# Expert tiles from an earlier point on, summary copies ahead of loads, and one exponential over two PSUM banks in a fused attention and mixture-of-experts kernel

## The chip, the cores and the metric

The kernel runs on one core of a Trainium2 chip. The metric is the device time of one execution in microseconds (us), lower is better. With one core there are no two dies to compare, so "slow" here only marks a run that is over 1.5% above the fastest run of the same kernel in its set of runs; all others are "fast". Executions of one kernel scatter by up to 4% within a set, and chips differ, so kernels are compared through ratios to the kernel before in the same set of runs. A ratio is the mean time of one kernel's fast runs over the mean of the other's fast runs of the same rounds, so it is not quite the ratio of the medians that stand beside it.

## The reference, cut to what matters

```python
# attention: q, k, v are (4, 8, 768, 64)
k_sum = k.reshape(B, H, 24, 32, D).max(axis=3)      # a summary of each block of 32 keys
v_sum = v.reshape(B, H, 24, 32, D).mean(axis=3)
# scores to the keys nearer than 16, and to the 24 summaries (+ log 32); one softmax over both
...
# mixture of experts on the 3072 tokens, width 512, 8 experts, hidden width 1024
logits = x @ w_gate + modality_bias[modality_id]
e_idx = np.argmax(logits, axis=1)
...
for e in range(E):
    h = np.maximum(x[mask] @ w1[e], 0.0)
    out[mask] = gate_w[mask, None] * (h @ w2[e])
```

## The kernel before

The program walks over 16 pairs of heads, four to a batch. After the last pair of a batch the batch is routed: each token gets its expert and a row in a DRAM buffer `xs` sorted by expert, and six indirect DMAs (scatters) write the tokens there. A "list" then names tiles of 256 rows with one expert. A tile is a generator; one step of it is a "unit", and `UNITS` says at which of six places of a pair one unit is run between attention work. What no unit took is run after the last pair (the tail).

```python
def scores(n, half):
    ...
    pss = [bank([128, 6, 64], FP32, f"pss{h}") for h in range(2)]   # one of 8 shared banks each
    ...
    for h in range(2):
        nc.scalar.activation(pT[:, h], pss[h], AF.Exp, scale=SCALE)

def tick(m=1):                       # one of 8 places in a pair
    ticks[0] += 1
    if ticks[0] % 2 == 0:
        scatter()                    # one scatter at every second tick
    for _ in range(m):               # m steps of the route
        while side and next(side[0], side) is side:
            side.popleft()

def rows(lst, j, i):                 # rows of tile i, issued by SP
    ...
    nc.sync.dma_start(xr.bitcast(I32), xs[ds(row, 256)].rearrange(...))

def weights(lst, j, i):              # the tile's expert, if another one than is there
    ...
    load_weights(i % NWB, e, cond=go > 0)        # both matrices, issued by GpSimd

def weights_ahead(n):                # guessed experts of tiles 0 and 1, by halves p0 to p7
    for p in {n + 2: (n,) for n in range(8)}.get(n, ()):
        ...
        if p == 3:
            guessed[0] = 1
        if p == 7:
            guessed[0] = NTILE + NWB
            ahead()                              # calls weights() of tile 1

for n in range(np_):
    scores(n, 1)
    tick(2 if n >= 8 else 1)
    pump(u[0])                                   # a unit of a tile, or none
    keys(n + 2)                                  # its halo copies on GpSimd
    ...                                          # at the first pair of a batch: start its route
    load(n + 4)                                  # three DMA issues on GpSimd
    weights_ahead(n)
    ...
    values(n, 0)
    ...
    summaries(n + 2)                             # two DVE reductions, one copy on GpSimd
    ...
    queries(n + 2); blocks(n + 1); scores(n + 1, 0); features(n - 1); values(n, 1)
    if n in ENLIST:                              # (7, 10, 14)
        scatter(NC)
        enlist(lists[b - 1])                     # row loads, weights
```

The softmax here doesn't subtract the row's maximum and nothing guards it: scores larger than these inputs give would overflow.

Of the kernel before, what the change touches and what calls it, by code (L numbers as in the profile page):

```python
# [10 lines left out]
FP32 = mybir.dt.float32  # L11
I32 = mybir.dt.int32
U32 = mybir.dt.uint32
AF = mybir.ActivationFunctionType
# [8 lines left out]
def kernel(  # L23
# [12 lines left out]
    nc = tc.nc  # L36
# [27 lines left out]
    ctx.enter_context(tc.manual_schedule())  # L64

    def bank(shape, dt, name):
        return ps.tile(shape, dt, tag="b", bufs=8, name=name)


    NMASK = 9  # L70
    NV, NK = 6, 3
    kvs = [const.tile([128, 2, NT, 128], FP16, name=f"kv{i}") for i in range(NK)]
    vbs = [const.tile([128, NT, 2, D + 1], FP16, name=f"vb{i}") for i in range(NK)]
# [26 lines left out]

    def borders(i):
        kv, vb = kvs[i], vbs[i]
        nc.vector.memset(kv[:, :, 0, 64:80], 0.0)
        nc.vector.memset(kv[:, :, NT - 1, 80:96], 0.0)
        nc.vector.memset(kv[:, :, :, KR:128], 0.0)
        nc.vector.memset(vb[0:WK, :, :, D:D + 1], 1.0)
        nc.vector.memset(vb[WK:KR, :, :, D:D + 1], 32.0)

    borders(0)
    tok = const.tile([128, NJ], I32, name="tok")  # L110
    nc.gpsimd.iota(tok, pattern=[[128, NJ]], base=0, channel_multiplier=1)
    midc = const.tile([NJ, 128], mybir.dt.int64, name="midc")
    mb0 = const.tile([128, 2, E], FP32, name="mb0")
    nc.sync.dma_start(mb0, moe_modality_bias.unsqueeze(0).to_broadcast([128, 2, E]))
# [44 lines left out]
    w1b = [wpool.tile([128, NCD, F], FP16, name=f"w1b{i}") for i in range(NWB)]  # L159
    w2b = [wpool.tile([128, NF, DM], FP16, name=f"w2b{i}") for i in range(NWB)]  # L160
    guess = const.tile([128, NWB], I32, name="guess")

    def early_constants():
        nc.vector.tensor_scalar(erev, cidx[:, 0:E], -1.0, float(E), op0=ALU.mult, op1=ALU.add)
        g1 = work.tile([128, 2], FP32, tag="g1", bufs=1, name="g1")
        nc.vector.reduce_max(g1, mb0, axis=AX.X)
        nc.vector.memset(exl, -1.0)
        yield

        g2 = work.tile([128, 2, E], FP32, tag="g2", bufs=1, name="g2")  # L170
        nc.vector.tensor_tensor(g2, mb0, g1.unsqueeze(2).to_broadcast([128, 2, E]), op=ALU.is_ge)
        nc.vector.memset(done, 0.0)
        nc.vector.tensor_tensor(g2, g2, erev[:, None, :].to_broadcast([128, 2, E]), op=ALU.mult)
        yield
        nc.vector.reduce_max(g1, g2, axis=AX.X)
        nc.vector.memset(ones, 1.0)
        nc.vector.tensor_tensor(exl[:, 0:1], g1[:, 0:1], g1[:, 1:2], op=ALU.max)
        nc.vector.tensor_tensor(exl[:, 1:2], g1[:, 0:1], g1[:, 1:2], op=ALU.min)
        yield
        nc.vector.tensor_scalar(exl[:, 0:2], exl[:, 0:2], -1.0, float(E), op0=ALU.mult, op1=ALU.add)  # L180
        nc.vector.tensor_copy(guess, exl[:, 0:2])
        yield

    def later_constants():
        nc.vector.tensor_scalar(erow, cidx[:, 0:E], float(RP), 256.0, op0=ALU.mult, op1=ALU.add)
        nc.vector.memset(xrs[-1], 0.0)
        nc.sync.dma_start(xs[0:256].rearrange("(a p) d -> p a d", p=128), xrs[-1].bitcast(I32))
        yield
        nc.gpsimd.dma_start(wg, moe_w_gate.rearrange("(c p) e -> p c e", p=128))
        yield  # L190
        nc.vector.tensor_scalar(upper, cidx, pidx, None, op0=ALU.is_gt)
        nc.vector.tensor_copy(prow[:, 0:1], pidx)
        nc.vector.tensor_scalar_add(prow[:, 1:2], pidx, 128.0)
        yield
        nc.vector.tensor_scalar_mul(k256, cidx[:, 0:KM].unsqueeze(2).to_broadcast([128, KM, E]), 256.0)
        nc.vector.tensor_tensor(rowc, k256, erow[:, None, :].to_broadcast([128, KM, E]), op=ALU.add)
        yield
        nc.vector.tensor_copy(tab[:, 2], cidx[:, None, 0:E].to_broadcast([128, KM, E]))
        mdiff = work.tile([128, E], FP32, tag="mdiff", bufs=1, name="mdiff")
        nc.vector.tensor_tensor(mdiff, mb0[:, 1, :], mb0[:, 0, :], op=ALU.subtract)  # L200
        yield
        mh = work.tile([NJ, 128], FP16, tag="mh", bufs=1, name="mh")
        nc.vector.tensor_copy(mh, midc.bitcast(I32)[:, 0::2])
        for _ in range(4):
            yield
        pm = bank([128, NJ], FP16, "pm")
        nc.tensor.transpose(pm, mh, ident[0:NJ, 0:NJ])
        yield
        midf = work.tile([128, NJ], FP32, tag="midf", bufs=1, name="midf")
        nc.vector.tensor_copy(midf, pm)  # L210
        yield
        nc.vector.tensor_tensor(base, midf.unsqueeze(2).to_broadcast([128, NJ, E]),
                                mdiff[:, None, :].to_broadcast([128, NJ, E]), op=ALU.mult)
        yield
        nc.vector.tensor_tensor(base, base, mb0[:, 0:1, :].to_broadcast([128, NJ, E]), op=ALU.add)
# [48 lines left out]
    def blocks(n):  # L264

        kv, vb = st[n]["kv"], st[n]["vb"]
        for half in range(2):
            pv = bank([128, 6, 128], FP16, "pv")
            for tl in range(6):
                nc.tensor.transpose(pv[:, tl, :], kv[:, 1, 6 * half + tl, :], ident)  # L270
            (nc.vector.tensor_copy if half or n < NMASK and n % 2 else nc.scalar.copy)(  # L271
                vb[0:KR, 6 * half:6 * half + 6, :, 0:D],
                pv[0:KR].rearrange("p t (h d) -> p t h d", h=2))

    def scores(n, half):
        s = st[n]
        qT, kv = s["qT"], s["kv"]
        pss = [bank([128, 6, 64], FP32, f"pss{h}") for h in range(2)]
        if n < NMASK:
            for h in range(2):  # L280
                nc.tensor.matmul(pss[h], ident, bterm[:, 6 * half:6 * half + 6, :],
                                 start=True, stop=False, skip_group_check=True)
        for tl in range(6):
            t = 6 * half + tl
            for h in range(2):
                rr = slice(64 * h, 64 * h + 64)
                nc.tensor.matmul(pss[h][:, tl, :], kv[rr, 0, t, :],  # L287
                                 qT[rr, ts(t, 8), :].rearrange("p s c -> p (s c)"),
                                 start=n >= NMASK, stop=True, skip_group_check=True)
        pT = work.tile([128, 2, 6, 64], FP16, tag="pT", bufs=3, name="pT")  # L290
        for h in range(2):
            nc.scalar.activation(pT[:, h], pss[h], AF.Exp, scale=SCALE)  # L292
        if n >= NMASK:
            nc.vector.tensor_tensor(  # L294
                pT[0:WK], pT[0:WK],
                bmask[0:WK, None, 6 * half:6 * half + 6, :].to_broadcast([WK, 2, 6, 64]), op=ALU.mult)
        s["pT", half] = pT
# [254 lines left out]



    UNITS = {9: "000111", 10: "101111", 11: "111111", 12: "101111", 13: "111111", 14: "111111", 15: "101111"}
    ENLIST = (7, 10, 14)
    todo, pending, heads = deque(), deque(), set()
    ended, guessed = [0], [0]

# [50 lines left out]

    def weights_ahead(n):

        for p in {n + 2: (n,) for n in range(8)}.get(n, ()):
            if p % 4 == 0:
                gv[p // 4] = nc.gpsimd.value_load(guess[0:1, p // 4:p // 4 + 1], min_val=0, max_val=E - 1)
            load_weights(p // 4, gv[p // 4], which=(p // 2 % 2,), part=p % 2)
# [4 lines that stand above are left out]
                ahead()  # L621
# [1 line left out]
    keys(0)  # L623
    summaries(0)
    load(2)
    borders(1)
    queries(0)
    scores(0, 0)
    blocks(0)
    keys(1)  # L630
    summaries(1)
    load(3)
    borders(2)
    queries(1)
    side.append(early_constants())
    side.append(later_constants())
    for n in range(np_):
        b, cc = pairs[n]
        u = [int(c) for c in UNITS.get(n, "000000")]
        scores(n, 1)  # L640
        tick(2 if n >= 8 else 1)
        pump(u[0])
        if n + 2 < np_:
            keys(n + 2)
        if n and cc == 0:
            features(n - 1)
            assert not side
            side.append(route(b - 1))
        if n + 4 < np_:
            load(n + 4)  # L650
        weights_ahead(n)
        tick(2 if n >= 8 else 1)
        pump(u[1])
        values(n, 0)
        tick(2 if n >= 8 else 1)
        if n + 2 < np_:
            summaries(n + 2)
        tick(2 if n >= 8 else 1)
        pump(u[2])
        if n + 2 < np_:  # L660
            queries(n + 2)
        tick(2 if n >= 8 else 1)
        pump(u[3])
        if n + 1 < np_:
            blocks(n + 1)
            tick(2 if n >= 8 else 1)
            scores(n + 1, 0)
        tick(2 if n >= 8 else 1)
        pump(u[4])
        if cc:  # L670
            features(n - 1)
        tick(2 if n >= 8 else 1)
        values(n, 1)
        tick(2 if n >= 8 else 1)
        if n in ENLIST:
            assert not side
            scatter(NC)
# [55 lines left out]
```

## Time and profile before

| | before |
|---|---|
| time, median of the first set of runs | 233.67 us (233.24 to 236.83, 4 runs) |
| span of the profiled run | 228.3 us |
| busy: PE, DVE, ACT, POOL | 184.0, 122.8, 119.4, 124.9 us |
| PE busy share | 81% |
| first expert matmul | 86.12 us |
| last features of attention | 155.15 us |

A pair is read from its second score matmuls to those of the next pair. Pair 7 starts at 58.69 us, and 79.8 us remain from the start of pair 15 to the end. The lengths of the pairs and the views are in the prediction below. No engine but TensorE is busy for more than 55% of the span; that is an average, and before 91 us single stretches are fuller (VectorE 8.99 of 9.30 us from 44.8 us on, DMA engines at a share of about 1).

### The profile page before, as it was taken

The page shows a single profiled execution, that of the slowest core. Times are in us where ns is not written, and L with a number is a line of the kernel's source. Part 1 is how long each engine was busy: PE and PEld are TensorE (multiplying, and loading weights), DVE is VectorE, ACT ScalarE, POOL GpSimd, SP SyncE. Part 2 cuts the span into 40 slices and gives each one's busy share as a digit, 9 for nine tenths or more (in the row PEclk, how much of TensorE's full clock was granted, in tenths as well). Part 3 has the DMA queues.
Part 4 walks back from the last instruction along what each step waited for, and adds up shares of the span by engine and source line. Part 5 has one row for each costly group of instructions (what it writes and reads, how often), then busy time and mean ns, then how long its engine had stood idle before and what let it go on. Part 6 is the DMA issues. An engine that isn't in the chain of part 4 may idle for free. (4 is left out here: it accounts for less than half of the span.)

```text
span 228.3 us, 6765 instructions
## 1 busy us (share of the span) xinstructions
PE 184.0 (81%) x2720; PEld 131.5 (58%) x2720; DVE 122.8 (54%) x352; ACT 119.4 (52%) x207; POOL 124.9 (55%) x198
## 2 busy tenths in 40 slices
PE   0676797869696549999789999999959899999900
PEld 0464575667465536766577667576626667766500
DVE  6369979699958994655449763534870111101000
ACT  2586568576854441867457675462424255554410
POOL 8459529738889180498531575311574757372220
PEclk9999589967977575999999999999997999999985
DMA  5979929999999999139950123241121434312100
GB/s 76 136 106 139 188 44 143 187 205 172 203 221 153 227 172 160 37 88 207 200 198 3 70 100 136 81 143 47 69 103 56 157 118 141 112 51 83 52 19 0
DMA packets 20090, 27.44 MB, mean 120 GB/s; under 512 B 2876, under 2 KB 16468, under 8 KB 20052
## 3 DMA queue, kind: packets, MB, share of 16 engines
q0 software_dynamic: 17424, 24.40, 52.8%
q1 hardware_dynamic: 2628, 2.54, 4.0%
q8 instruction: 23, 0.38, 0.7%
q14 instruction: 15, 0.12, 0.2%
HBM read 85.46 MB, written 10.44 MB: 420 GB/s over the span
## 5 line engine op out<-in xcount | busy, mean ns | idle before, releaser
L530 PE MATMUL ph<-xg,w1b 128*128 128x256 f16 x416 | 53.8, 285 | 6.6 <-DVE at L516 3.8
L530 PEld LDWEIGHTS <-w1b 128*128 128x128 f16 x416 | 40.4, 101 | 14.9 <-issue 7.0
L542 PE MATMUL pmo<-w2b,hT 128*128 128x512 f16 x208 | 48.5, 379 | 0.0
L548 POOL DMA_INDIRECT out_dram<-ot,at x26 | 25.9, 997 | 32.8 <-ACT ot L547 22.3
L292 ACT ACTIVATE pT<-pss 128x384 f16<-128x384 f32 x64 | 28.0, 495 | 23.5 <-PE pss L287 23.4
L533 ACT ACTIVATE hT<-ph 128x512 f16<-128x512 f32 x52 | 30.6, 602 | 17.2 <-PE ph L530 16.7
L547 ACT ACTIVATE ot<-pmo,xr 128x512 f32<-128x512 f32 x26 | 17.9, 688 | 27.7 <-PE pmo L542 18.0
L351 POOL DMA_INDIRECT xs<-xb,posi x24 | 24.9, 1040 | 13.1 <-issue 5.3
L542 PEld LDWEIGHTS <-hT 128*128 128x128 f16 x208 | 19.2, 98 | 20.6 <-ACT hT L533 1.4
L238 ACT COPY kv<-pk 128x768 f16<-128x768 f16 x32 | 24.3, 810 | 8.1 <-PE pk L237 7.8
L513 DVE COPY xg<-px 128x1024 f16<-128x1024 f16 x13 | 8.9, 686 | 34.0 <-PE px L511 34.0
L270 PE MATMUL pv<-ident,kv 128*128 128x128 f16 x192 | 16.0, 244 | 4.0 <-POOL kv L251 4.0
L318 DVE TENSOR_TENSOR xb<-po,rec 128x384 f16<-128x384 f32 x32 | 17.8, 557 | 1.0
L241 POOL COPY kv<-kv 128x352 f16<-128x352 f16 x16 | 7.9, 493 | 18.7 <-ACT kv L238 18.5
L270 PEld LDWEIGHTS <-kv 128*128 128x128 f16 x192 | 13.5, 110 | 5.7 <-POOL kv L251 4.4
L248 DVE TENSOR_REDUCE ks<-kv 128x24 f16<-128x768 f16 x16 | 15.1, 944 | 2.2 <-ACT kv L238 2.2
L250 DVE TENSOR_REDUCE ks<-kv 128x24 f16<-128x768 f16 x16 | 15.1, 943 | 0.8 <-ACT kv L238 0.8
L294 DVE TENSOR_TENSOR pT<-pT,bmask 96x768 f16<-96x768 f16 x14 | 8.5, 604 | 13.2 <-ACT pT L292 13.2
L330 DVE COPY xT<-pt 128x768 f16<-128x768 f16 x16 | 8.9, 555 | 12.0 <-PE pt L327 11.8
L271 DVE COPY vb<-pv 120x768 f16<-120x768 f16 x20 | 10.7, 551 | 7.4 <-PE pv L270 7.4
L261 ACT COPY qT<-pq 128x768 f16<-128x768 f16 x16 | 12.9, 809 | 3.0 <-PE pq L259 2.9
L287 PEld LDWEIGHTS <-kv 64*128 64x128 f16 x384 | 8.4, 101 | 10.4 <-issue 8.9
(127 smaller groups left out, 280.7 us busy)
## 6 DMA issues: line engine op xcount, KB each, us to landing
w1b<-in_moe_w_dram POOLq DMA_DIRECT2D x13, 1024.0 KB
w2b<-in_moe_w_dram POOLq DMA_DIRECT2D x13, 1024.0 KB
kn<-in_k_dram POOLq DMA_DIRECT2D x16, 192.0 KB
vn<-in_v_dram POOLq DMA_DIRECT2D x16, 192.0 KB
qn<-in_q_dram POOLq DMA_DIRECT2D x16, 192.0 KB
xr<-xs SPq DMA_DIRECT2D x8, 272.0 KB, 7.1
w1b<-in_moe_w_dram POOLq DMA_DIRECT2D x4, 512.0 KB
w2b<-in_moe_w_dram POOLq DMA_DIRECT2D x4, 512.0 KB
```

The source lines that it names most:

```text
L238: nc.scalar.copy(kv[:, i, :, 0:64].rearrange("p t (s c) -> p t s c", c=C8), bass.AP(pk.tensor, pk.offset, [pk.ap[0], [8, NT], [1, 8], [P8, ...
L248: nc.vector.reduce_max(ks[:, 0], kv[:, 0, :, 0:64].rearrange("p t (g s) -> p t g s", g=2), axis=AX.X)
L250: nc.vector.reduce_sum(ks[:, 1], kv[:, 1, :, 0:64].rearrange("p t (g s) -> p t g s", g=2), axis=AX.X)
L270: nc.tensor.transpose(pv[:, tl, :], kv[:, 1, 6 * half + tl, :], ident)
L292: nc.scalar.activation(pT[:, h], pss[h], AF.Exp, scale=SCALE)
L318: nc.vector.tensor_tensor(xo, po[:, :, :, 0:D], rec.unsqueeze(3).to_broadcast([128, 2, 3, D]), op=ALU.mult)
L351: apart("xs", nc.gpsimd.indirect_dma_start(out=xs[:, :], out_offset=bass.IndirectOffsetOnAxis(ap=posi[:, c:c + 1], axis=0), in_=xb[:, c, : ...
L530: nc.tensor.matmul(ph[:, f, :], w1[:, c, ts(2 * f2 + f, 128)], xg[:, c, :], start=(c == 0), stop=(c == NCD - 1))
L533: nc.scalar.activation(hT[:, 2 * f2:2 * f2 + 2, :], ph, AF.Relu)
L542: nc.tensor.matmul(po, hT[:, f, ts(s2, 128)], w2[:, f, :], start=(f == 0), stop=(f == NF - 1))
L547: nc.scalar.activation(ot, po, AF.Copy, scale=gt)
L548: apart("out", nc.gpsimd.indirect_dma_start(out=out[:, :], out_offset=bass.IndirectOffsetOnAxis(ap=at[:, s2:s2 + 1], axis=0), in_=ot[:], i ...
```

## The change

It wants to fill TensorE where it idles, from 58 to 91 us, with expert work that stands later, and to take small waits out of the early pairs: the list of batch 0 is taken a pair earlier, units start in pair 7 instead of 9, the last half of tile 1's guessed weights is fetched a pair earlier, summary copies are queued ahead of loads on GpSimd, two exponentials become one over two banks, the mask is a multiplication from pair 7 on, all first halves of v go to ACT, and border memsets go to GpSimd.

```diff
-        return ps.tile(shape, dt, tag="b", bufs=8, name=name)
+        return ps.tile(shape, dt, tag="b", bufs=4, name=name)
-    NMASK = 9
+    NMASK = 7
 ... (borders(): five memsets, and three others, from nc.vector to nc.gpsimd, all at the start)
-            (nc.vector.tensor_copy if half or n < NMASK and n % 2 else nc.scalar.copy)(
+            (nc.vector.tensor_copy if half else nc.scalar.copy)(
-        pss = [bank([128, 6, 64], FP32, f"pss{h}") for h in range(2)]
+        two = ps.tile([128, 2, 512], FP32, tag="s", bufs=2, name="pss")[:, :, 0:384]
+        pss = [two[:, h].rearrange("p (t s) -> p t s", s=64) for h in range(2)]
-        for h in range(2):
-            nc.scalar.activation(pT[:, h], pss[h], AF.Exp, scale=SCALE)
+        nc.scalar.activation(pT.rearrange("p h t s -> p h (t s)"), two, AF.Exp, scale=SCALE)
-    UNITS = {9: "000111", 10: "101111", 11: "111111", 12: "101111", 13: "111111", 14: "111111", 15: "101111"}
-    ENLIST = (7, 10, 14)
+    UNITS = {7: "000111", 8: "001110", 9: "010101", 10: "010101",
+             11: "111110", 12: "101111", 13: "111110", 14: "101111", 15: "101110"}
+    ENLIST = (6, 10, 14)
-        for p in {n + 2: (n,) for n in range(8)}.get(n, ()):
+        for p in {2: (0,), 3: (1,), 4: (2,), 5: (3,), 6: (4,), 7: (5,), 8: (6, 7)}.get(n, ()):
 ... (route steps per tick: T = (1, 2, 2, 2) by batch, so two from pair 4 on instead of pair 8;
      one step less before an early transpose, range(4) to range(3))
-        if n + 4 < np_:
-            load(n + 4)
-        weights_ahead(n)
 ... (one tick, one unit, values(n, 0), one tick)
         if n + 2 < np_:
             summaries(n + 2)
+        if n + 4 < np_:
+            load(n + 4)
+        weights_ahead(n)
```

More of the change, by code (lines that the diff above doesn't have):

```diff
@@ L102, in borders @@
         kv, vb = kvs[i], vbs[i]
-        nc.vector.memset(kv[:, :, 0, 64:80], 0.0)
-        nc.vector.memset(kv[:, :, NT - 1, 80:96], 0.0)
-        nc.vector.memset(kv[:, :, :, KR:128], 0.0)
-        nc.vector.memset(vb[0:WK, :, :, D:D + 1], 1.0)
-        nc.vector.memset(vb[WK:KR, :, :, D:D + 1], 32.0)
-    borders(0)
+        nc.gpsimd.memset(kv[:, :, 0, 64:80], 0.0)
+        nc.gpsimd.memset(kv[:, :, NT - 1, 80:96], 0.0)
+        nc.gpsimd.memset(kv[:, :, :, KR:128], 0.0)
+        nc.gpsimd.memset(vb[0:WK, :, :, D:D + 1], 1.0)
+        nc.gpsimd.memset(vb[WK:KR, :, :, D:D + 1], 32.0)
     tok = const.tile([128, NJ], I32, name="tok")
     nc.gpsimd.iota(tok, pattern=[[128, NJ]], base=0, channel_multiplier=1)
+    for i in range(NK):
+        borders(i)
     midc = const.tile([NJ, 128], mybir.dt.int64, name="midc")
@@ L161 @@
     guess = const.tile([128, NWB], I32, name="guess")
+    nc.gpsimd.memset(exl, -1.0)
+    nc.gpsimd.memset(done, 0.0)
+    nc.gpsimd.memset(ones, 1.0)
     def early_constants():
@@ L166, in early_constants @@
         nc.vector.reduce_max(g1, mb0, axis=AX.X)
-        nc.vector.memset(exl, -1.0)
         yield
@@ L171, in early_constants @@
         nc.vector.tensor_tensor(g2, mb0, g1.unsqueeze(2).to_broadcast([128, 2, E]), op=ALU.is_ge)
-        nc.vector.memset(done, 0.0)
         nc.vector.tensor_tensor(g2, g2, erev[:, None, :].to_broadcast([128, 2, E]), op=ALU.mult)
@@ L175, in early_constants @@
         nc.vector.reduce_max(g1, g2, axis=AX.X)
-        nc.vector.memset(ones, 1.0)
         nc.vector.tensor_tensor(exl[:, 0:1], g1[:, 0:1], g1[:, 1:2], op=ALU.max)
@@ L203, in later_constants @@
         nc.vector.tensor_copy(mh, midc.bitcast(I32)[:, 0::2])
-        for _ in range(4):
+        for _ in range(3):
             yield
@@ L625 @@
     load(2)
-    borders(1)
     queries(0)
@@ L632 @@
     load(3)
-    borders(2)
     queries(1)
@@ L636 @@
     side.append(later_constants())
+    T = (1, 2, 2, 2)
     for n in range(np_):
@@ L640 @@
         scores(n, 1)
-        tick(2 if n >= 8 else 1)
+        tick(T[b])
         pump(u[0])
@@ L648 @@
             side.append(route(b - 1))
+        tick(T[b])
+        pump(u[1])
+        values(n, 0)
+        tick(T[b])
+        if n + 2 < np_:
+            summaries(n + 2)
         if n + 4 < np_:
@@ L651 @@
         weights_ahead(n)
-        tick(2 if n >= 8 else 1)
-        pump(u[1])
-        values(n, 0)
-        tick(2 if n >= 8 else 1)
-        if n + 2 < np_:
-            summaries(n + 2)
-        tick(2 if n >= 8 else 1)
+        tick(T[b])
         pump(u[2])
@@ L661 @@
             queries(n + 2)
-        tick(2 if n >= 8 else 1)
+        tick(T[b])
         pump(u[3])
@@ L665 @@
             blocks(n + 1)
-            tick(2 if n >= 8 else 1)
+            tick(T[b])
             scores(n + 1, 0)
-        tick(2 if n >= 8 else 1)
+        tick(T[b])
         pump(u[4])
@@ L671 @@
             features(n - 1)
-        tick(2 if n >= 8 else 1)
+        tick(T[b])
         values(n, 1)
-        tick(2 if n >= 8 else 1)
+        tick(T[b])
         if n in ENLIST:
```

## The prediction

> **What bounds the kernel now.** I read the activity slices of the page first, then busy time in chosen stretches, then the instructions of TensorE and GpSimd in order of time. The slices:
>
> ```profile
> PE   0676797869696549999789999999959899999900
> PEclk9999589967977575999999999999997999999985
> DMA  5979929999999999139950123241121434312100
> ```
>
> Each digit is 5.7 us. From slice 16 (91 us) on, PE is full at full clock; before it, PE is partly idle, and in several slices the granted clock is near half. Busy time by stretch, cut at the second score matmuls of chosen pairs (columns: length, busy us of PE, PE weight load, DVE, ACT, POOL, then granted clock, DMA share, GB/s):
>
> ```profile
> 39.20:44.80 5.60, 5.00 (x145) 3.98 (x144) 3.39 (x11) 3.29 (x6) 4.18 (x8) 1.00 1.10 182
> 44.80:54.10 9.30, 7.50 (x131) 5.85 (x128) 8.99 (x26) 5.74 (x11) 5.77 (x10) 0.63 1.19 199
> 58.30:65.70 7.40, 4.89 (x120) 3.63 (x118) 6.61 (x13) 5.04 (x10) 6.42 (x8) 0.91 1.13 200
> 65.70:77.40 11.70, 7.18 (x155) 5.78 (x153) 8.30 (x27) 4.78 (x9) 9.31 (x17) 0.65 0.99 202
> 77.40:90.90 13.50, 9.72 (x143) 7.78 (x142) 10.47 (x29) 5.25 (x9) 4.60 (x8) 0.63 1.11 176
> 101.60:114.70 13.10, 11.65 (x171) 7.82 (x170) 6.21 (x13) 7.99 (x14) 9.84 (x16) 1.00 0.94 192
> ```
>
> No engine fills 58 to 91 us: chains of waits set it. From 91 us PE sets it. Two batches' routes (choosing experts for tokens) and the first experts' weights fall into the same stretch. The PE instructions before 91 us with waits in brackets:
>
> ```profile
> 37.01 0.84 PE L270 MATMUL pv<-ident,kv 128*128 128x128 f16 x12 [1.30 <-POOL kv L251]
> ...
> 63.07 0.84 PE L270 MATMUL pv<-ident,kv 128*128 128x128 f16 x12 [2.17 <-POOL kv L251]
> ...
> 76.78 0.19 PE L412 MATMUL pc<-tot,ones 128*128 128x8 f16 x1 [2.71 <-DVE tot L408]
> ...
> 86.12 1.87 PE L530 MATMUL ph<-xg,w1b 128*128 128x256 f16 x8 [3.78 <-DVE at L516]
> ...
> 110.81 0.62 PE L511 MATMUL px<-ident,xr 128*128 128x128 f16 x8 [1.45 <-DMA xr<-xs]
> ```
>
> The reader is to see that PE stands at v's transposes for the summary copy, at the route for DVE, and once for gathered rows. GpSimd before the 2.17 us wait:
>
> ```profile
> 58.22 0.71 POOL L83 DMA_DIRECT2D kn<-in_k_dram  x1
> 58.92 0.69 POOL L83 DMA_DIRECT2D vn<-in_v_dram  x1
> 59.58 0.66 POOL L83 DMA_DIRECT2D qn<-in_q_dram  x1
> 60.21 0.75 POOL L224 DMA_DIRECT2D w1b<-in_moe_w_dram  x1
> 61.26 1.07 POOL L351 DMA_INDIRECT xs<-xb,posi  x1 [0.30 <-DVE rec L311]
> 62.30 0.71 POOL L251 COPY kv<-ks 128x576 f16<-128x576 f16 x1
> ```
>
> The copy's input was ready at 59.65 (end of the second DVE reduction); it started 2.65 us later, behind issues.
>
> **What the Trainium skill says.** (1) Perfetto Trace Analysis, Optimization Strategy: where the most-contended engine changes over time, "performance may be improved by interleaving those regimes". The slices show such regimes. (2) TensorE: Matmul & The Clock Gate, Part 1: a PE that idles is gated to half rate. Agrees: granted 0.63 to 0.65 in two stretches with PE waits, 1.00 where PE is full. Hence filling idle PE also speeds the work already there. (3) ScalarE: Activation LUTs, What ACT_TABLE_LOAD costs: an ACTIVATE with immediates costs 186 ns plus 0.833 ns per element, neighbours overlapping by about 93 ns. Agrees: 495 ns at 384 elements against 506. (4) Perfetto Trace Analysis, Matmul Optimizations: use all 8 PSUM banks. The new kernel still allocates 8, but 4 are tied to scores; no run yet shows what that costs.
>
> **The change part by part.**
>
> *Exponential.* 64 of 128x384 become 32 of 128x768. ReLU at 512 elements takes 602 ns, so the slope is (602-495)/128 = 0.84 ns per element and one of 768 costs about 495+384x0.84 = 816 ns; two back to back now span 870. That is 32x0.05 = 1.7 us of ACT, which is 52% busy: about 0 on the path. The two heads' matmuls alternate, so a common wait costs little.
>
> *v by ACT.* The four odd pairs below 9 move one copy each: +4x0.80 us ACT, -4x0.5 us DVE. Good in 58 to 66 us where DVE is 6.61 of 7.40; I give 0.5 us.
>
> *Mask.* Pairs 7 and 8 lose 8 mask matmuls (about 0.25 us each at full clock, from 0.50 for two: 2.0 us of PE) and gain 4 DVE multiplications of 0.6 us. In pairs now holding expert work, PE is the scarcer: -1 us.
>
> *Summary copies ahead of loads.* They lift three waits, 1.30+2.17+0.52 = 4.0 us, which is also the sum that the view of waits gives for v's transposes behind this copy. Some is taken over by DVE, whose reductions end just before: -2.5 us. Loads get later but are issued two pairs before use.
>
> *Border memsets to GpSimd.* 18 memsets before the first halo copy, which started at 8.69 after 2.9 us of idle. POOL copies of 352 and 576 elements take 0.48 and 0.67 us: slope 0.85 ns, intercept about 0.2 us. Estimate 18x0.2 = 3.6 us, 1 us more than the idle: +1 us at the start, and DVE is freed of as many near 10 and 16 us: -0.5.
>
> *Expert work earlier.* This is the large term. The digits of the schedule sum to 36 in both versions: 3+5+6+5+6+6+5 before, 3+3+3+3+5+5+5+5+4 after. So the same tiles remain for the tail, and the tail (155.7 to 228.3 us) stays as it is. A tile costs 7.39 us of PE there (starts at 187.50 and 194.90) for 6 units, 1.23 us each. Nine units now run by the end of pair 9, against 3: 6x1.23 = 7.4 us of PE moves out of the PE-bound stretch. Pair lengths before, from one pair's second scores to the next: pair 7 7.8, 8 10.9, 9 13.5, 10 10.7, 11 13.2, 12 12.1, 13 11.6, 14 10.0, 15 7.2. PE work of a pair without mask at full clock is about 3.3 us (sum of start-to-start times at 34 to 39 us less masks). So after:
> - pair 7: 3.3+3.7+0.5 = 7.5 if nothing waits;
> - pair 8, with the route: 3.3+3.7+1 = 8, say 8.7, as expert matmuls now stand between the route's matmuls;
> - pair 9: 7.0, say 8; pair 10: 7.5, say 8;
> - pairs 11, 13, 14 and 15 hold one unit less each (pair 12 holds 5 in both): -1.2 in each.
>
> Differences: -0.3, -2.2, -5.5, -2.7, -1.2x4 = -15.5 us.
>
> *What comes back.* Rows for the first tile. A row load starts only after all six scatters of its batch land (last scatter ended 66.8, load issued 69.9) and lands 3.5 to 9.0 us later, median 7.1. Before, the turn of tile 0 stood a pair and a half after the list was taken (80.2 us). Now the list is taken at the end of pair 6 and the turn comes half a pair later, with the last scatter early in pair 6: 3+7 us after it, against about 7 us of program. PE runs in order, so I put +4 us at pair 7. The same stands in pair 11, where tile 2's turn is now right behind the second scores: +2.5 over the 1.45 it paid. The route in pair 4 advances two steps per tick instead of one, so its PE steps follow DVE more closely, as in pair 8 before (2.71 us): +1.
>
> Sum: -0.5-1-2.5+1-0.5-15.5+4+2.5+1 = -11.5 us. 233.79-11.5 = 222.3. (The profiled run was shorter, 230.08 with a span of 228.3; I take the difference over to the median as it is.)
>
> **Rivals.** (a) *DMA becomes the bound.* DMA share is 1.0 to 1.2 at 176 to 202 GB/s from 39 to 91 us. Rates by stretch add up to about 10.4 MB there, and the new kernel needs nearly the same by the end of pair 8, plus one more half weight. At 200 GB/s that is 52 us after 33.6: 86 us, where the estimate has pair 9 ending near 84 to 87. Against: PE waited for inputs only in the first 23 us. If it binds, weights of tile 1 arrive late and GpSimd stands at them (it stood 7.4 us before), and the time is 228. (b) *Four banks are too few.* Pairs with experts use about 14 evictions on 4 banks where 18 shared 8; ACT once stood 4.25 us for its output buffer in the tail. With 1 us of PE stall in each of 9 pairs: 231. (c) *No row stall and PE full from pair 7:* the 6.5 us of stalls vanish and the clock holds: 215. (d) *Everything in the early pairs was slack of something else:* the copies' 2.5 us come back as DVE waits: 225.
>
> **Range and chances.** (c) and (a) bracket the likely: 214 to 229. Faster by over 2% means below 229.1; only (b), or (a) and (d) together, miss it: 0.85. Within 2%: 0.12. Slower by 2% needs bank stalls above 16 us: 0.03.
>
> **What will show it.** Right: the first expert matmul near 62 to 68 us instead of 86; no wait of v's transposes for the copy above 1 us; tile 0's row transposes waiting for the row load 2 to 6 us; granted clock near 1 from pair 7 on; 64 to 76 us from the last features to the end, as before (72.6). Wrong: PE waiting for evictions by ACT between expert matmuls (b); for weights or inputs from DMA (a); an attention phase whose end is later than 149 or earlier than 139 us.

## The result, and the profile after

The kernel became slower: 249.62 us median (247.83 to 251.67, 4 runs) against 233.67 us, ratio 1.066, 95% interval 1.053 to 1.080. The prediction had 222.3 us and a range up to 229. The profiled run, span 250.0 us, took 251.67 us, which is 1.55% above the kernel's fastest and so counts as slow by a hair; a second profile of the same kernel in another set of runs (below) shows the same waits.

Of the signs that the prediction named, the tail held (74.7 us, named 64 to 76). The first expert matmul came at 78.95 us (62 to 68 named), tile 0's row wait was 13.1 us (2 to 6), the clock in pair 7 fell to 0.53 (near 1), v's transposes once waited 3.78 us for the copy (1 at most), and the last features came at 175 us (139 to 149).

The engines' work hardly changed: busy 185.1 us on PE, 119.0 DVE, 119.8 ACT, 128.3 POOL; the loss is waiting. The activity slices of the kernel after, 6.25 us to a digit:

```profile
PE   1595988596007998754299989999896899999800
PEclk9998699979555999967579999999997999999975
DMA  5769869999999049355864321233122343312100
```

TensorE has a hole where the change wanted it full: slices 10 and 11 (62.5 to 75 us) are empty and the clock is at half. A second dip is in slices 18 and 19 (112 to 125 us). The busy times by stretch of the kernel after, cut as before (length; busy us of PE, weight load, DVE, ACT, POOL; granted clock, DMA share, GB/s):

```profile
58.85:63.05 4.20, 2.06 (x77) 1.63 (x72) 2.93 (x8) 2.91 (x4) 3.59 (x5) 1.00 1.07 144
63.05:76.27 13.22, 0.07 (x5) 0.01 (x1) 1.88 (x3) 0.80 (x1) 8.91 (x16) 0.53 1.01 202
76.27:82.44 6.17, 6.17 (x66) 4.97 (x68) 3.02 (x7) 2.21 (x3) 0.00 (x0) 0.63 0.90 164
82.44:92.21 9.77, 9.21 (x181) 7.05 (x181) 7.46 (x26) 6.11 (x10) 3.60 (x7) 1.00 0.09 10
...
115.25:135.38 20.13, 12.17 (x165) 8.34 (x164) 4.95 (x10) 7.27 (x11) 10.74 (x19) 0.75 0.54 134
```

The first three lines are pair 7: it takes 23.6 us instead of 7.8. For 13.22 us nothing runs on TensorE, ACT or DVE but 2.75 us of leftovers, while GpSimd is busy for 8.91 us; then TensorE runs its backlog without a gap but at 0.63 of full clock. The last line is pair 11, 20.1 us instead of 13.2. The longest waits of TensorE after, in order of time:

```profile
76.27 1.04 PE L512 MATMUL px<-ident,xr 128*128 128x128 f16 x8 [13.14 <-DMA xr<-xs]
...
108.91 1.46 PE L271 MATMUL pv<-ident,kv 128*128 128x128 f16 x12 [3.78 <-POOL kv L252]
...
123.53 1.03 PE L512 MATMUL px<-ident,xr 128*128 128x128 f16 x8 [7.94 <-DMA xr<-xs]
```

Before, these row transposes (`px`) waited 1.45 us once, for tile 2, and not at all for tile 0. The load of tile 0's rows, as SP issues it (the first of the two issues in each line), kernel after and kernel before:

```profile
67.79 1.59 SPq L489 DMA_DIRECT2D xr<-xs  x2
...
69.90 1.58 SPq L488 DMA_DIRECT2D xr<-xs  x2
```

Why it is not earlier is seen on GpSimd, kernel after, in order of time:

```profile
52.87 1.03 POOL L352 DMA_INDIRECT xs<-xb,posi  x1 [0.16 <-issue]
54.48 0.66 POOL L252 COPY kv<-ks 128x576 f16<-128x576 f16 x1 [0.59 <-DVE ks L251]
55.09 0.71 POOL L83 DMA_DIRECT2D kn<-in_k_dram  x1
...
57.08 0.81 POOL L225 DMA_DIRECT2D w2b<-in_moe_w_dram  x1
58.19 1.05 POOL L352 DMA_INDIRECT xs<-xb,posi  x1 [0.30 <-issue]
...
63.60 0.99 POOL L352 DMA_INDIRECT xs<-xb,posi  x1 [0.17 <-issue]
```

The six scatters of batch 0 start at 50.63, 52.87, 58.19, 59.55, 61.25 and 63.60 us. From 54.48 us on GpSimd rests only for some 0.3 us before a scatter: a copy, three loads and a weight half stand between the second scatter and the third. The last ends at 64.6. SP issues the row load at 67.79, once all six have landed, 3.2 us later, and it lands at 76.27, 8.5 us later. In the kernel before the issue was at 69.90: the change took the list a pair earlier, and the row load came only 2.1 us earlier. TensorE, which takes its instructions in order, reached the row transposes at 63.1 us instead of 80.2 and had to stop. The Trainium skill, Trainium Architecture — The Big Picture, section Inside one NeuronCore, says that each engine has its own instruction stream and program counter and that they meet only through semaphores. That agrees: being earlier in the program made TensorE earlier, and did nothing for GpSimd.

For tile 2, again GpSimd of the kernel after:

```profile
92.01 1.51 POOL L225 DMA_DIRECT2D w2b<-in_moe_w_dram  x2
93.77 0.04 POOL L225 DMA_DIRECT2D w1b<-in_moe_w_dram  x1 [0.25 <-DMA w1b<-in_moe_w_dram]
102.70 0.04 POOL L225 DMA_DIRECT2D w2b<-in_moe_w_dram  x1 [8.89 <-DMA w2b<-in_moe_w_dram]
103.69 1.07 POOL L352 DMA_INDIRECT xs<-xb,posi  x1 [0.95 <-DVE rec L312]
```

The conditional load of tile 1's second matrix writes where the guessed halves p6 and p7 are still arriving, so GpSimd stands 8.89 us for them. All six scatters of batch 1, and the summary copy that TensorE waits 3.78 us for, stand behind it. The row load of tile 2 is issued at 120.0 and TensorE stops for 7.94 us.

By pairs the two profiles differ as follows (us, after minus before): pair 7 +15.8; 8 −1.2; 9 −4.7; 10 +3.6; 11 +7.0; 12 +1.1; 13 and 14 −0.9 each; from pair 15 to the end +1.8. With +0.2 until pair 7 this is the 21.7 us between the spans.

### The profile page after: what moved, and what is told of

It is laid out like the page before. It is cut to its first block, busy times and chain, and to the rows that moved or that the text cites. A ratio compares the mean times of both kernels' runs of the same rounds, so it can differ in the third digit from the quotient of the medians.

```text
span 250.0 us, 6723 instructions
## 1 busy us (share of the span) xinstructions
PE 185.1 (74%) x2712; PEld 130.8 (52%) x2712; DVE 119.0 (48%) x334; ACT 119.8 (48%) x179; POOL 128.3 (51%) x216
## 5 line engine op out<-in xcount | busy, mean ns | idle before, releaser
L543 PE MATMUL pmo<-w2b,hT 128*128 128x512 f16 x208 | 51.4, 397 | 0.1
L534 ACT ACTIVATE hT<-ph 128x512 f16<-128x512 f32 x52 | 30.4, 599 | 12.9 <-PE ph L531 12.3
L293 ACT ACTIVATE pT<-pss 128x768 f16<-128x768 f32 x32 | 26.1, 820 | 20.9 <-PE pss L289 20.5
L543 PEld LDWEIGHTS <-hT 128*128 128x128 f16 x208 | 20.2, 101 | 22.3 <-issue 3.5
L352 POOL DMA_INDIRECT xs<-xb,posi x24 | 25.3, 1054 | 10.9 <-issue 5.7
L512 PE MATMUL px<-ident,xr 128*128 128x128 f16 x104 | 9.0, 233 | 22.1 <-DMA xr<-xs 21.1
L272 ACT COPY vb<-pv 120x768 f16<-120x768 f16 x16 | 13.1, 816 | 21.3 <-PE pv L271 21.3
L271 PE MATMUL pv<-ident,kv 128*128 128x128 f16 x192 | 17.3, 248 | 6.1 <-POOL kv L252 3.8
L252 POOL COPY kv<-ks 128x576 f16<-128x576 f16 x16 | 10.7, 671 | 17.6 <-DVE ks L251 14.6
L512 PEld LDWEIGHTS <-xr 128*128 128x128 f16 x104 | 7.1, 104 | 23.1 <-DMA xr<-xs 21.3
L271 PEld LDWEIGHTS <-kv 128*128 128x128 f16 x192 | 14.4, 112 | 8.1 <-POOL kv L252 4.1
```

Source lines behind the costliest of these rows:

```text
L271: nc.tensor.transpose(pv[:, tl, :], kv[:, 1, 6 * half + tl, :], ident)
L293: nc.scalar.activation(pT.rearrange("p h t s -> p h (t s)"), two, AF.Exp, scale=SCALE)
L352: apart("xs", nc.gpsimd.indirect_dma_start(out=xs[:, :], out_offset=bass.IndirectOffsetOnAxis(ap=posi[:, c:c + 1], axis=0), in_=xb[:, c, : ...
L512: nc.tensor.transpose(px[:, c, s2, :], xr[:, s2, ts(c, 128)], ident)
L534: nc.scalar.activation(hT[:, 2 * f2:2 * f2 + 2, :], ph, AF.Relu)
L543: nc.tensor.matmul(po, hT[:, f, ts(s2, 128)], w2[:, f, :], start=(f == 0), stop=(f == NF - 1))
```

## The experiments

**Units and list alone, on both kernels.** The kernel after with the old `UNITS` and `ENLIST` (a1; it keeps the new route steps), and the kernel before with the new ones and what they need in route steps (b1).

```diff
 # a1, on the kernel after
-    UNITS = {7: "000111", 8: "001110", ...}      ENLIST = (6, 10, 14)
+    UNITS = {9: "000111", 10: "101111", ...}     ENLIST = (7, 10, 14)
 # b1, on the kernel before: the reverse, tick(2 if n >= 4 else 1), range(3) for range(4)
```

> The changed kernel with the old expert schedule (units from pair 9, lists taken at pairs 7, 10, 14); four rotating banks, one exponential, copies ahead of loads and memsets on GpSimd stay. Rows theory (TensorE stands at the row transposes of tiles 0 and 2 because they stand in its queue before the rows can land): the 13.1 us wait is gone and most of the 7.9 us, and with them the cold matmuls after; 226 to 233 us, at or below the kernel before. Banks theory (four rotating banks stall TensorE): still above 243. GpSimd theory (what was put on GpSimd, or both last weight halves in pair 8, holds it back): 236 to 243, with the wait for weights of about 9 us still there.

> The kernel before with the new expert schedule alone (units from pair 7, lists at pairs 6, 10, 14, two route steps per tick from batch 1 on, one step less before the transpose of the modalities); eight banks, split exponentials, loads ahead of copies, memsets on VectorE stay. Rows theory: 244 to 256 us, with a wait of 9 us or more at tile 0's row transposes. Banks theory and GpSimd theory: the schedule alone gains, 220 to 230.

Measured, with the kernel before at 236.89 us median in this set of runs: a1 237.2 us, ratio 1.009 (0.991 to 1.028); b1 261.64 us, ratio 1.117 (1.093 to 1.140). In b1 the row transposes of tiles 0 and 2 wait 15.60 and 10.80 us, in a1 neither waits. So the loss comes with the units and the list; the other parts together can't be told from no change (their interval reaches to 2.8%).

**The weights of tile 1.** The kernel after with half p7 back in pair 9.

```diff
-... 7: (5,), 8: (6, 7)}
+... 7: (5,), 8: (6,), 9: (7,)}          # all halves as the kernel before has them
```

> The changed kernel with the last half of the second expert's weights fetched in pair 9 again, not in pair 8. Rows theory: the 13.1 us wait of tile 0 stays, the time is within 3 us of the changed kernel (245 to 251). GpSimd theory: GpSimd is free for the second batch's scatters earlier, the wait of tile 2 (7.9 us) and that of v's transposes (3.8 us) go, and the time falls by 8 to 12 us, to about 238.

Measured: 257.25 us, ratio 1.094 (1.073 to 1.116). Tile 0 waits 11.26 us, tile 2 only 3.21, but TensorE now waits 8.03 us for tile 1's first matrix. Its halves had been issued by pair 7, but tile 1's conditional load stands behind p7 in GpSimd's program and was reached only at 104.35 us; right after it GpSimd stood 6.48 us for the second matrix. The wait changed its place and the time stayed.

**A scatter at every tick.**

```diff
-        if ticks[0] % 2 == 0:
-            scatter()
+        scatter()
```

> The changed kernel with one scatter at every tick instead of every second, so the six scatters of a batch are issued sooner in GpSimd's order. Rows theory: tile 0's wait falls by the advance of the last scatter, 3 to 6 of 13.1 us, tile 2's by 1 to 4; time 239 to 245. Banks theory: no change, 247 to 250.

Measured: 254.18 us, ratio 1.080 (1.056 to 1.103). Tiles 0 and 2 wait 9.95 and 4.13 us, but v's transposes wait 6.87 us for a summary copy. The last scatter of batch 0 started at 63.02 us, 0.6 us earlier than in the kernel after: between scatters GpSimd still has the loads and weight halves of the pairs. A finer pace in the program isn't an earlier place in GpSimd's queue. The rows came no earlier: SP issued their load at 69.50 us, 5.5 us after the end of the last scatter (3.2 in the kernel after), and they landed at 76.98 us. Tile 0's wait is shorter because TensorE reached it later, at 67.0 us instead of 63.1. So this lever failed, and the run doesn't test what an earlier last scatter is worth; a5 below does.

**The same kernel again, and units without pair 7.** The kernel after unaltered, and a version (a4) that takes no unit in pair 7 and makes up for it later, again 36 in all.

```diff
-    UNITS = {7: "000111", 8: "001110", 9: "010101", 10: "010101",
-             11: "111110", 12: "101111", 13: "111110", 14: "101111", 15: "101110"}
+    UNITS = {8: "000111", 9: "010101", 10: "011101",
+             11: "111111", 12: "101111", 13: "111110", 14: "111111", 15: "101110"}
```

> The changed kernel itself, unaltered, beside the others on one chip, since this chip's times need not be those of the first. All theories: 1.06 to 1.08 of the kernel before, with the waits of 13 and 8 us at the row transposes.

> The changed kernel with the same 36 units of expert work, but none in pair 7: three in pair 8, three in 9, four in 10, then 6, 5, 5, 6, 4. Lists are still taken at pair 6. Rows theory: TensorE reaches tile 0's row transposes about 8 us later, after more useful work, so that wait falls from 13 to 0 to 5 us, and tile 2's row transposes stand two slots later, so its wait falls to under 4: 228 to 238 us, at most 0.95 of the changed kernel. Rivals (four banks, GpSimd's extra work): within 3 per cent of the changed kernel.

Measured, the kernel before at 238.21 us median: the kernel after 256.65 us, ratio 1.090 (1.068 to 1.113), its two row waits 11.77 and 7.96 us in a fast run; a4 240.38 us, ratio 1.026 (1.006 to 1.046). In a4 the row waits are 1.74 and 1.30 us. So with the waits most of the loss goes, from 9.0% to 2.6%. But a4 gains nothing either, and the prediction owed 11 us. At pair 11 a4 was ahead of the first profile of the kernel before by 1.6 us and two units; pair 8 took 14.5 us though it held only three units, and pairs 11 and 12 took 16.2 and 14.3. Its busy times in pairs 8 and 11:

```profile
67.83:82.33 14.50, 11.06 (x176) 8.97 (x173) 10.19 (x34) 5.54 (x8) 9.39 (x17) 0.56 1.14 205
...
99.95:116.13 16.18, 13.35 (x172) 8.52 (x172) 6.50 (x13) 7.68 (x12) 13.18 (x21) 0.89 0.87 204
```

In pair 8 the DMA share is 1.14 and the clock 0.56; in pair 11 GpSimd is busy 13.18 of 16.18 us. In a4, too, GpSimd had stood 8.58 us for p6 and p7.

**The banks, and the copies, alone on the kernel before.**

```diff
 # b2: bufs=4 for the shared banks, two tiles of two banks for scores, one exponential, as in the change
 # b3: summaries(n + 2) ahead of load(n + 4) and weights_ahead(n), as in the change
```

> The kernel before with the PSUM split and the one exponential alone: four rotating banks, two score tiles of two banks. Rows theory with my prediction's account (1.7 us of ACT saved off the path, small bank waits): within 1 per cent of the kernel before. Banks theory: 3 per cent slower or more, with TensorE waiting for evictions by ACT.

> The kernel before with the summary copies ahead of the loads (and of the fetches of weights) on GpSimd alone. My prediction's account: the three waits of v's transposes for this copy (4.0 us) go, 1 to 3 us faster. GpSimd theory: loads and weights that now stand behind the copy's own wait for VectorE come late, and the time is the same or up to 2 per cent longer.

Measured in the same set of runs: b2 236.96 us, ratio 1.011 (0.992 to 1.031); b3 233.52 us, ratio 0.998 (0.976 to 1.020). Neither is distinguishable from 1. The bank rival is not what made the kernel slower. In b3 the copy's three waits are gone, and it reaches pair 8 at 63.03 us against 66.46 in the first profile (another chip, so only roughly): a lead of 3.4 us, more than the 2.5 predicted. Pair 8 then takes 16.0 us instead of 10.9. TensorE's longest wait in it is for VectorE in the route,

```profile
74.88 0.20 PE L386 MATMUL pr<-oh,upper 128*128 128x48 f16 x1 [3.23 <-DVE oh L378]
```

where it was 0.69 us before, with another 1.67 us for a load of k. In this one profile it went as rival (d) had said: the copies' gain came back as waits for VectorE.

**Small parts alone on the kernel before.** Memsets on GpSimd, mask from pair 7 on, v by ACT (diff as in the change).

> The kernel before, with the change's small parts alone: the border memsets and three others on GpSimd, the mask as a multiplication from pair 7 on, and the first half of v always copied out by ACT. The prediction had +1 for the memsets, -0.5 for DVE, -0.5 for v by ACT and -1 for the mask: -1.0 us in all, ratio 0.996. Theory from the runs so far: every kernel reaches pair 7's second scores at 58 to 59 us whatever is done early, so the ratio is 0.99 to 1.01. Rival: the memsets delay the start and this is not taken up by later slack: 1.01 or more.

Measured: 231.54 us median of 5 runs, three of them fast (229.67, 230.05, 231.54). The kernel before had 235.6 us median of 7 in that set of runs, but only one run, 229.44, counts as fast, so no interval can be given; fast against fast it is 1.004. No gain or loss is shown; with one fast run of the kernel before, neither theory is decided. The first theory's ground, that every kernel reaches pair 7 at 58 to 59 us, does not hold: a3 had reached it at 62.4 us, and b4 itself did at 56.7.

**Scatters in one go.** The kernel after with all six scatters as soon as the places are known. In the same set of runs: weight halves of tile 1 later (a6), and the units of a4 on eight shared banks (c1).

```diff
 # a5, on the kernel after
-        if b == B - 1:
-            scatter(NC)
+        scatter(NC)
 # a6, on the kernel after
-... 5: (3,), 6: (4,), 7: (5,), 8: (6, 7)}
+... 5: (3,), 8: (4, 5), 9: (6, 7)}
 # c1: the kernel before with b3, v by ACT, the mask, and UNITS, ENLIST and route steps of a4
```

> The kernel after, with the six scatters of a batch issued in one go as soon as their places are known, instead of one at every second tick. Theory: tile 0's row load starts 3.2 us after the last scatter, and the last scatter is late because GpSimd puts copies, loads and weight halves between the scatters (50.6 to 64.6 us in the kernel after). In one go six scatters need about 6 x 1.3 = 8 us, so the last ends near 58.5 instead of 64.6, the load is issued near 61.7 instead of 67.8, and the wait of tile 0's row transposes falls from 13.1 to 6 to 8 us; the summary copy of that pair is held up by some us, which may return a part. Time 2 to 3 per cent below the kernel after (ratio to the kernel before about 1.06, if the kernel after is 1.09 of it). Rival: the row load lands late because of the other transfers, whenever it is issued: then landing grows to more than 10 us and the wait stays above 10. Then the time stays within 1 per cent of the kernel after.

> The kernel after, with the halves p4 and p5 of the second expert's weights issued in pair 8 and p6 and p7 in pair 9, so that none of them shares the DMA engines with tile 0's rows. Theory: the row load needs 8 to 9 us from issue to landing because the DMA engines are full (share above 1.0) then; with 1 MB less in the queue it lands in 4 to 6 us, and the wait of tile 0's row transposes falls from 13.1 to 8 to 10. Tile 1 starts in pair 9 and will stand for its first matrix's halves, which are issued a pair before it, for 3 to 8 us, so the time is about that of the kernel after or longer (ratio to the kernel before 1.07 to 1.12). Rival: the landing is set by the load itself (256 rows, one queue): it stays at 8 us or more.

> The kernel before, with summary copies ahead of loads, the first half of v by ACT, the mask as a multiplication from pair 7 on, the list taken in pair 6, two route steps per tick from pair 4 on, and the expert units of the run with the later turn (none in pair 7, three in pair 8). It keeps eight banks that are shared and two exponentials. It tells whether the four banks are why the run with the later turn, which led the kernel before by about 4 us at pair 11, lost it again in pairs 11 and 12. If the banks are the reason: ratio 0.97 to 0.99, the first kernel to beat the kernel before. Rival: the loss there comes from GpSimd and the weights of tiles 2 and 3, which are asked for no earlier than before: ratio 1.01 to 1.03 again.

The kernel before: 235.6 us median of 7 runs, one of them fast (229.44), so ratios are rough here; the runs of the three kernels were on the same chip.

a5: 239.05 us median; its two fast runs, 235.57 and 238.81, are 1.03 of the one fast run of before, where the kernel after was 1.07 and 1.09 in two other sets of runs. The scatters run from 48.80 to 56.36 us, the row load is issued at 59.23 instead of 67.79, and tile 0's row transposes, reached at 65.85 us, don't wait for it at all, where I had expected 6 to 8 us of the wait to stay. Pair 7 takes 10.0 us instead of 23.6. This kernel reaches pair 10 at 89.58 us with nine units done; the kernel before reached it at 90.85 with three. That lead of 1.3 us and six units of 1.23 us are 8.7 us, a good part of the gain that the prediction wanted (its terms up to there come to a lead of 6.5 us and the same six units). Then pair 10 takes 19.8 us. GpSimd and TensorE of a5 in it:

```profile
91.83 0.04 POOL L225 DMA_DIRECT2D w2b<-in_moe_w_dram  x1 [9.37 <-DMA w2b<-in_moe_w_dram]
92.83 1.06 POOL L352 DMA_INDIRECT xs<-xb,posi  x1 [0.95 <-DVE rec L312]
...
102.42 0.68 POOL L252 COPY kv<-ks 128x576 f16<-128x576 f16 x1
```

The last line above is preceded, left out, by five more scatters, two halo copies and an output; TensorE's next wait is

```profile
103.16 1.46 PE L271 MATMUL pv<-ident,kv 128*128 128x128 f16 x12 [9.40 <-POOL kv L252]
```

The hold of GpSimd is the same as in the kernel after; only what waits behind it changed.

a6: 250.57 us median, as slow as the kernel after (its fast runs are 1.09 of the one fast run of before). Its profiled run counts as slow by a hair, at 1.50% above its fastest. Its waits of TensorE:

```profile
71.65 1.04 PE L512 MATMUL px<-ident,xr 128*128 128x128 f16 x8 [7.90 <-DMA xr<-xs]
100.53 1.87 PE L531 MATMUL ph<-xg,w1b 128*128 128x256 f16 x8 [8.57 <-DMA w1b<-in_moe_w_dram]
123.32 1.03 PE L512 MATMUL px<-ident,xr 128*128 128x128 f16 x8 [9.12 <-DMA xr<-xs]
```

Its row load was issued at 68.22 us, so it landed in 3.4 us instead of 8.5. While it was under way the engines moved 3.43 us x 194 GB/s = 0.67 MB; in the kernel after 8.48 us x 200 GB/s = 1.70 MB. The difference is 1.03 MB, just the two halves p4 and p5. So the long landing was what shared the DMA engines with the load (p4 was issued just before it, p5 4.3 us after it), not the load itself. The 5 us came back at once as a wait for the weights that had been put off. The Trainium skill, DMA: Bandwidth & Descriptors, section Anatomy of one DMA, fits one DMA that GpSimd issues as 2.0 us plus its bytes over 436e3. For the row load's 272 KB that is an estimate of 2.6 us (SP issues it, so the fit is only a yardstick): it is near the 3.4 us of a6 and far from the 8.5 us with more beside it.

c1: 238.66 us median, 1.04 of the one fast run of before. GpSimd stood 7.75 us for a weight half there, and tile 2 waited 8.13 us for its rows. Eight banks didn't help. The ratio lies even above the rival's 1.01 to 1.03, and GpSimd's part in it is as the rival had it.

**The hold taken away.** The kernel after with a5's scatters and tile 1's conditional load split in two (a7): its second matrix's part comes at a unit in pair 10, when the halves have landed. The wait itself stays, so nothing is read or written early. Beside it the same on eight banks with two exponentials (a8), the split without a5's scatters (a9), and a5's scatters on the kernel before (b5).

```diff
     def weights(lst, j, i):
         ...
-        load_weights(i % NWB, e, cond=go > 0)
+        load_weights(i % NWB, e, which=(0,) if i == 1 else (0, 1), cond=go > 0)
+        if i == 1:
+            rest[i] = (e, go)
 ... in expert_tile, after a ReLU
+            if f2 == 2 and i in rest:
+                e, go = rest.pop(i)
+                load_weights(i % NWB, e, which=(1,), cond=go > 0)
```

> The kernel after with scatters in one go, as in the run before, and tile 1's conditional load split: its second matrix's part is issued at tile 1's third unit (pair 10), when the guessed halves have long landed, instead of in pair 8, where GpSimd stood 9.4 us for them. Theory: in the run with scatters in one go the kernel led the kernel before at pair 10 by 1.3 us and nine units, and lost it in pair 10 (19.8 us), where v's transposes waited 9.4 us for a summary copy behind GpSimd's hold and the second batch's six scatters. With the hold gone pair 10 takes 10 to 12 us, no wait of PE is longer than 6 us, and the span is 224 to 229: 4 per cent below the run with scatters in one go, ratio to the kernel before 0.96 to 0.985. Rival: the six scatters in one go alone hold the copy back (8 us of GpSimd), or tile 2's rows and weights bind then: pair 10 stays above 15 us or pair 11 grows, and the ratio stays at 1.00 or more.

> The same with eight shared banks and two exponentials again. If the four banks and the common exponential cost nothing, as the run of these alone had it (ratio 1.01, not distinguishable from 1), it is within 1 per cent of the kernel with the split hold. Rival: with expert work from pair 7 on the four banks stall TensorE by about 1 us in each pair: then it is 2 per cent or more faster.

> The kernel after with the split hold alone, scatters at every second tick as in it. Theory: tile 0's wait of 13 us stays; tile 2's (7.9 us) and the 3.8 us of the copy go, as batch 1's scatters are no longer behind the hold: 6 to 11 us less than the kernel after, ratio to the kernel before 1.03 to 1.05. Rival: tile 2's wait has its own cause (the pace of the scatters), and stays above 5 us: ratio 1.06 or more.

> The kernel before with scatters in one go alone. There the row load of tile 0 is issued 10 us ahead of its use, so an earlier one gains nothing, and the summary copies behind six scatters come up to 6 us later. Theory: ratio 1.00 to 1.03. Rival: early scatters help by themselves (the DMA engines are filled more evenly): 0.98 or less, and then the gain in the run with scatters in one go was not the row wait.

Measured, the kernel before at 234.53 us median of 10 runs:

| | median us | ratio of fast runs | 95% |
|---|---|---|---|
| a7 split and scatters in one go | 227.55 | 0.978 | 0.971 to 0.986 |
| a8 the same, eight banks | 227.71 | 0.979 | 0.972 to 0.985 |
| a9 split only | 243.3 | 1.047 | 1.037 to 1.057 |
| b5 scatters in one go, kernel before | 232.34 | 0.999 | 0.991 to 1.007 |

a7 and a8 beat both kernels, by about 2% of the kernel before (the intervals say 1.4 to 2.9%). (The expectation of a7 speaks of a lead of nine units; it is nine units done against three.) a7's pair 10 takes 8.9 us in a profile of the slow group, a8's 10.8 in a fast one. a9 keeps tile 0's wait (12.80 us) and more of tile 2's than I expected (5.02 us): the two cures are needed together. b5 shows that early scatters gain nothing on the whole where no one waits for rows; its v transposes wait 8.8 us for summary copies behind the scatters, against 4.0. a8's profile is from a fast run; its busy times in pairs 7 to 9:

```profile
61.11:73.44 12.33, 8.38 (x143) 7.08 (x140) 7.42 (x16) 5.43 (x9) 6.92 (x15) 0.62 1.14 206
73.44:82.91 9.47, 8.75 (x180) 6.77 (x179) 7.33 (x24) 6.14 (x12) 4.39 (x8) 1.00 0.83 128
82.91:91.20 8.29, 7.50 (x146) 5.34 (x140) 7.94 (x28) 6.22 (x11) 6.11 (x8) 1.00 1.12 164
```

Pairs 8 and 9 are near what the prediction sized (8.7 and 8). Pair 7, sized at 7.5 us, takes 12.3: the DMA share is 1.14 at 206 GB/s, the clock is 0.62, and TensorE's longest wait there is

```profile
67.53 0.85 PE L260 MATMUL pq<-ident,qn 96*64 96x96 f16 x16 [3.50 <-DMA qn<-in_q_dram]
```

a wait for the load of q of pair 9. In the program it stands two pairs ahead. GpSimd issues it here at

```profile
59.30 0.66 POOL L83 DMA_DIRECT2D qn<-in_q_dram  x1
```

which is 1.8 us before TensorE begins pair 7, behind the six scatters in one go (48.93 to 56.49 us); the kernel before issued it at 52.20 us. So this wait has two parts, a late issue and then 7.6 us until it lands in full DMA engines. The scatters also hold back a summary copy: v's transposes wait 3.42 us for it at 58.05 us, and a5, a7 and a8 begin pair 7 at 61.0 to 61.9 us instead of 58.7. And one hold of GpSimd is left: for the second matrix of tile 0 it stands 5.26 us, to 70.43 us. The cure has costs of the kind that it cures; no run takes them away.

## Why the prediction was wrong, point by point

- **What comes back, rows of the first tile (+4 us): the step that failed.** The mechanism was named and the size was off by 9 us: 13.1 us. I had put the last scatter "early in pair 6", where the program has it. GpSimd ran late and ended it at 64.6 us, 5.8 us after TensorE had begun pair 7. The other terms, 3+7 us from there to the landing, measured 3.2+8.5. On top, TensorE came out of the wait at 0.63 of its clock: 6.17 us of full work in 76.27 to 82.44 us would be, as an estimate, 3.9 at full clock (6.17x0.63), so some 2.3 us more. The prediction had hoped that filling TensorE speeds the work already there; in this stretch TensorE is full and still slow. (Its own views were less even than it read them: 0.63 to 0.65 stands in three stretches, not two, and from 58.3 to 65.7 us TensorE was busy for 66% at a clock of 0.91.) a5 shows the cause of the wait: with the scatters earlier on GpSimd the wait is gone.
- **The same in pair 11 (+2.5 us)** measured 7.9 us, with 3.8 us for the copy in pair 10. Rival (a) had said that GpSimd would stand at weights of tile 1. It did, 8.89 us, but I had let it cost the weights' user and not the scatters and copies behind it on the same engine. a7 against a5 shows it: without the hold pair 10 takes 8.9 us (94.38 to 103.27, a slow run; 10.8 in a8, a fast one) instead of 19.8.
- **Expert work earlier (-15.5 us)** was partly right. In the kernel after pairs 8 and 9 gave −1.2 and −4.7 (prediction −2.2 and −5.5). With both cures (a7) the whole kernel is 0.978 of the kernel before, which is 5 us, not 11.5. In a8 pairs 7 to 14 take 83.6 us against 89.8 before (two chips, so only roughly); the estimate gave −14.3 for them. Pair 7 alone falls short by 4.8 us (12.3 against 7.5): TensorE idles for 3.95 us of it, 3.50 of them for q's load, and works at 0.62 of its clock. The DMA rival has a part in this, and so has the late issue by GpSimd; how much each isn't shown. Where the rest of the difference went isn't settled.
- **The tail.** From the last features to the end it was to stay at 72.6 us and measured 74.7 after (175.32 to 250.0), 75.0 in a8 and 73.2 before, counted alike from the last features. I had also taken one unit's 1.2 us out of pair 15; from its start to the end it is 1.8 us longer. I made no run for these 2 us; they stay open.
- **Summary copies (-2.5 us), v by ACT, mask, memsets.** b3 and b4 can't be told from 1, but the intervals and the single fast run leave room for terms of this size. Pair 7 starts at 58.69 before and 58.85 after, so nothing is won by then; only one of the copy's three waits (1.30 us, at 37.01) lies before it, however. For the other two b3 is the better witness, and in its one profile their gain came and went again in pair 8, as rival (d) had it. The exponential was sized well (820 ns measured, 816 estimated).
- **Four banks (rival b)** cost nothing measurable: a7 and a8 are within 0.1% of each other, and b2 is 1.011 (0.992 to 1.031).
- **The range.** I had bounded slower outcomes by bank stalls above 16 us alone and gave them 0.03. Two stalls on the path of TensorE, each sized from the order of the program, were the risk, and I did not widen the range for it.

## What to carry to other kernels

When work is moved earlier on an engine that takes its instructions in order, ask for each input when the engine that produces it will get there by the clock, not where it stands in the program: here the row load moved ahead by 2.1 us when its user moved ahead by 17. An engine that only issues transfers is on the critical path as soon as one of its waits stands ahead of another's input; a conditional load over a buffer that is still being filled is such a wait, and putting it off from pair 8 to pair 10, together with scatters in one go, made the change pay. Test a group of changes by its scheduling part alone first: b1 showed the loss, and more than it, in one run.

## What the Trainium skill lacked or had wrong

- Perfetto Trace Analysis, Optimization Strategy, advises interleaving regimes with different limits. It lacks the caution that interleaved work brings its waits into an in-order queue: here TensorE did 0.07 us of work in 13.2 us, and the same idea gave 1.066 with the two waits for rows and 0.978 without them.
- DMA: Bandwidth & Descriptors, Anatomy of one DMA, gives a fixed 2.0 us and a rate for one DMA. The fit has no term for what else is under way: the same 272 KB row load landed in 3.4 us (a6) and 8.5 us (kernel after, DMA share 1.08 at 200 GB/s). Nor was its rate reached: the halves p6 and p7, 1 MB, are an estimate of 4.4 us by the fit and landed 9.2 us after the second issue. The engines had been nearly idle before (share 0.09), with only three loads of 192 KB just ahead, and were then full (share 1.01) at 146 GB/s.
- The same section calls the generation of descriptors small and variable, and gives no figure for an indirect scatter. Here 24 scatters of 128 rows keep GpSimd for a mean of 1054 ns each in the kernel after (how much of that is descriptors the trace doesn't say), and six in one go take 7.6 us of its queue (48.80 to 56.36 us in a5).
